# Attention with a routed feed-forward layer on one core: a sum of the first plan stands later on VectorE, and the plan's last steps and four scatters of the fifth batch stand at the end of pair 29

## The chip, the cores and the metric

The kernel runs on one core of a Trainium2 chip. The metric is the device time in microseconds (us) of one execution. Next to it stands a profile of one execution: which engine ran what, when, and what it waited for.

## What is computed

The reference, cut to what matters:

```python
def _attn_ref(q, k, v):                      # (8 batches, 8 heads, 576 tokens, 64), float32
    q_rot, k_rot = rotate(q), rotate(k)      # rotary embedding
    scores = np.matmul(q_rot, k_rot.transpose(0, 1, 3, 2)) / np.sqrt(D)
    attn = softmax(scores)
    return np.matmul(attn, v)

def _moe_ref(x, modality_id, w_gate, modality_bias, w1, w2):   # x: (4608, 512)
    logits = x @ w_gate + modality_bias[modality_id]           # 8 experts
    e_idx = np.argmax(logits, axis=1)                          # one expert for a token
    gate_w = softmax(logits)[np.arange(N), e_idx]
    for e in range(E):
        mask = e_idx == e
        h = np.maximum(x[mask] @ w1[e], 0.0)                   # w1[e]: 512 x 1024
        out[mask] = gate_w[mask, None] * (h @ w2[e])           # w2[e]: 1024 x 512
```

The attention's output, as 4608 rows of 512, is the input `x` of the second function.

## The kernel before

**Attention, 32 pairs.** Two heads are worked on together, so there are 32 pairs, and four pairs make a batch: pairs 16 to 19 are the fifth batch (number 4). For each pair the two rotated halves of q and k are loaded into one of two buffers `R` (`ST1` for even pairs, `ST2` for odd ones; the profile calls both ST), GpSimd multiplies them with cosine and sine and adds them (`rope_`, parts 0 to 2, lines 466 to 470), ScalarE rounds the sum to a high part (part 3, the HI step, a copy at L457) and GpSimd subtracts this to get the low part (part 4, the LO step, L474). Both stand in `HL`. Two copies for each of the two parts then write the other order of the two heads to `SW` (`swap`, L482): four DMAs for a pair, two that need HI and two that need LO. TensorE multiplies scores from `HL` and `SW` (L497), VectorE takes row minima and moves the scores out of PSUM (L506), ScalarE makes exponentials (L515), TensorE transposes them (L520), VectorE and ScalarE copy them out (L553 and L457), and TensorE multiplies them with V (L578). Even and odd pairs have a buffer each for `HL`, `SW`, `R` and V, so pair 31 takes the buffers that pair 29 had.

**Routing.** After the last pair of a batch, `route` finds each token's expert and its row in the expert's part of a DRAM table `XS`. The batch's output rows, in DRAM as `X`, are loaded back in five pieces (`back`, written BK0 to BK4, L761 and L763) into two buffers `XL`, used in turn, and each piece is scattered to `XS` by an indirect DMA that GpSimd issues (`scatter`, SC0 to SC4, L743). Since there are two buffers, the third load waits until the first scatter has read its buffer. For the first five batches the loads stand in SyncE's queue, for later ones in GpSimd's.

**The first plan.** When five batches are scattered, `plan0` decides which blocks of 512 rows are complete for an expert, and five blocks are worked off while the other batches are still being routed. The plan is a chain of small operations on one partition. Most are GpSimd's; its sums (`total`, L788) are VectorE's. `plan0` is a generator, cut by `yield` into steps.

**Experts.** The rows of a block are loaded (`m_ix`, `m_rows`), transposed and multiplied with the two weight matrices (`m_l1`, L1089; `m_plain`, `m_super`; L1207 and L1331). From there on TensorE works without a break to the end.

**What sets the order.** Each step is an entry of a list with a number; the list is sorted by it, and the engines' instructions are written in that order. The number of a step of pair n is 14.438 n plus an entry of the tables `KEYS` and `EDGE[n]`; that of a step of the expert part is 14.438 times 31 plus an entry of `MOE`. The numbers set the order alone; every engine runs its own row of instructions strictly in this order and waits where a buffer or a value is not there. SyncE issues nearly all loads, in the same order. So an instruction that waits holds up all that stands behind it on its engine.

Of the kernel before, what the change touches and what calls it, by code (L numbers as in the profile page):

```python
# [25 lines left out]
NSB = 4  # L26
NA = 1 + NSA
NB_MAX = 20
# [102 lines left out]
        "LD1": -42.214,  # L131
    },
    19: {
        "BK0": 71.4, "BK1": 71.5, "BK3": 95.0, "BK2": 116.0, "BK4": 131.0,
        "SC3": 113.825, "SC2": 128.215, "SC4": 152.075,
    },
# [73 lines left out]
    setdma=(-399.9101, -371.7589, -36.5660, -104.6596),  # L210
    consts=(-3.3332, 30.1765),
    plan=(-34.727, -25.884, -5.857, 16.183),
    ix=(-13.525, 11.679, 11.775, 17.3),
    w1=(-33.501, -27.735, 15.231, -22.655),
    w2=(-4.011, 1.762, 12.647, -8.483),
    hi=(-22.046, 1.027, 19.87, 16.903),
# [8 lines left out]
    l1d=(22.8091, 22.8691, 24.6621, 24.6471),  # L225
    w1n=(20.502, 24.643, 23.254, 22.825),
    place=(14.247, 18.005),
    rows=(-13.5, 11.7, 20.6, 31.756, 31.757),
    pl=(-114.356, -102.856, -99.906, -88.406, -85.506, -73.956, -51.417, -48.907, -45.303),
    end=24.98,  # L230
)
PIN = "PE,Activation,DVE,Pool"
# [3 lines left out]
def tile_attention_moe(ctx: ExitStack, tc: tile.TileContext, qk, v, mod, wg, mb, w1, w2, rope, cf, ci, out):  # L236
# [19 lines left out]
    PLA = cst.tile([1, 3, NA], I32, name="PLA")  # L256
    PLB = cst.tile([1, 3, NSB + NB_MAX + 1], I32, name="PLB")
# [6 lines left out]
    def cview(name):  # L264
        o, n = CF_OFF[name]
        return CF[:, o:o + n]
# [121 lines left out]
    def setup():  # L388
        g = nc.gpsimd
        v_ = nc.vector  # L390
        v_.memset(EPS, 1e-9)
        v_.memset(ZERO, 0.0)
        for t in PD:
            v_.memset(t, 0.0)
        v_.memset(P4, 0.0)
        for t in Vs:
            v_.memset(t[64:128, 0, 4, :], 0.0)
            v_.memset(t[0:64, 1, 4, :], 0.0)
        v_.memset(G, 0.0)
        for t in HL + SW:  # L400
            for c in (0, TW - 64):
                v_.memset(t[:, :, c:c + 64].bitcast(F32), 0.0)
        for h in range(4):
            for s in range(2):
                g.tensor_copy(RW[s * 64:s * 64 + 64, h, :].rearrange("p (o c) -> p o c", o=2)[:, :, 0:32],
                              idf[s * 64:s * 64 + 64, s * 64:s * 64 + 64].rearrange("p (o c) -> p o c", o=2))
        g.memset(MI, 0)
        nonlocal TI
        TI = XG[0].rearrange("p t g f -> p (t g f)")[:, 0:XU]
        g.memset(TI, 0.0)  # L410
        for x in XL:
            g.memset(x[:, XU:XW], 0.0)
        g.memset(TI[:, DM:DM + 1].bitcast(I32), EMPTY)
        g.memset(ON, 1.0)
        g.memset(OH, 0.0)
        g.dma_start(out=CF, in_=cf)
        g.dma_start(out=VAL, in_=ci)
# [363 lines left out]
    def plan0():  # L781
        G_ = nc.gpsimd

        def t1(name, sh):
            return sm.tile([1] + sh, F32, name=name, tag=name, bufs=1)

        def total(o, i):
            nc.vector.tensor_reduce(o, i, op=ALU.add, axis=AX.X)  # L788

        most = NPL * S // SUP  # L790
        AB = AB9[:, 0:E]
        sl = cview("SL")[0:1]
        EBv = cview("EB")[0:1]
        tri = cview("TRI")[0:1].rearrange("p (a b) -> p a b", b=E)
        nf, nb, cum, ge, tk, a2, rem, hc = (t1(x, [E]) for x in ("nf", "nb", "cum", "ge", "tk", "a2", "rem", "hc"))
        G_.tensor_tensor(nf, RUN[0:1, NPL, :], EBv, op=ALU.subtract)
        th = t1("th", [most])
        G_.tensor_scalar(th, sl[:, 0:most], float(SUP), float(SUP), op0=ALU.mult, op1=ALU.add)
        full = t1("full", [E, most])
        sh = [1, E, most]  # L800
        G_.tensor_tensor(full, nf.unsqueeze(2).to_broadcast(sh), th.unsqueeze(1).to_broadcast(sh), op=ALU.subtract)
        G_.tensor_scalar(full, full, 0.0, None, op0=ALU.is_ge)
        yield
        total(nb, full)
        yield
        t88 = t1("t88", [E, E])
        G_.tensor_tensor(t88, tri, nb.unsqueeze(1).to_broadcast([1, E, E]), op=ALU.mult)
        total(cum, t88)
        yield
        G_.tensor_tensor(tk, cum, nb, op=ALU.subtract)  # L810
        G_.tensor_scalar(tk, tk, float(NSA), None, op0=ALU.min)
        G_.tensor_scalar(a2, cum, float(NSA), None, op0=ALU.min)
        G_.tensor_tensor(a2, a2, tk, op=ALU.subtract)
        G_.tensor_scalar(hc, a2, float(SUP), None, op0=ALU.mult)
        G_.tensor_tensor(rem, nf, hc, op=ALU.subtract)
        G_.tensor_scalar(rem, rem, float(BLK), None, op0=ALU.is_ge)
        G_.tensor_tensor(t88, tri, rem.unsqueeze(1).to_broadcast([1, E, E]), op=ALU.mult)
        yield
        total(tk, t88)
        yield  # L820
        G_.tensor_scalar(tk, tk, 1.0, None, op0=ALU.is_equal)
        G_.tensor_tensor(rem, rem, tk, op=ALU.mult)
        G_.tensor_scalar(AB, a2, 2.0, None, op0=ALU.mult)
        G_.tensor_tensor(AB, AB, rem, op=ALU.add)
        sh = [1, NSA + 1, E]
        cmp = t1("cmp", [NSA + 1, E])
        cs = cmp[:, 1:NSA + 1, :]
        shs = [1, NSA, E]
        G_.tensor_tensor(cs, cum.unsqueeze(1).to_broadcast(shs), sl[:, 0:NSA].unsqueeze(2).to_broadcast(shs), op=ALU.subtract)
        G_.tensor_scalar(cs, cs, 0.0, None, op0=ALU.is_le)  # L830
        G_.tensor_tensor(cmp[:, 0, :], rem, cview("W8")[0:1], op=ALU.mult)
        yield
        es = t1("pes", [NB_MAX + 1])[:, 0:NA]
        total(es, cmp)
        yield
        G_.tensor_scalar(es[:, 0:1], es[:, 0:1], -1.0, float(E), op0=ALU.mult, op1=ALU.add)
        G_.tensor_scalar(es, es, float(E - 1), None, op0=ALU.min)
        G_.tensor_copy(PLA[:, 0, 0:NA], es)
        ch = t1("ch", [NB_MAX])[:, 0:NSA]
        G_.tensor_tensor(ch, es[:, 1:NA], es[:, 0:NSA], op=ALU.subtract)  # L840
        G_.tensor_scalar(ch, ch, 0.0, None, op0=ALU.is_equal)
        G_.tensor_scalar(PLA[:, 2, 1:NA], ch, -1.0, 1.0, op0=ALU.mult, op1=ALU.add)
        G_.memset(PLA[:, 2, 0:1], 1)
        G_.tensor_scalar(ge, nb, -float(SUP), float(RS), op0=ALU.mult, op1=ALU.add)
        G_.tensor_tensor(cs, cs, ge.unsqueeze(1).to_broadcast(shs), op=ALU.mult)
        G_.tensor_tensor(hc, hc, EBv, op=ALU.add)
        G_.tensor_scalar(hc, hc, float(-E * RS), None, op0=ALU.add)
        G_.tensor_tensor(cmp[:, 0, :], hc, rem, op=ALU.mult)
        yield
        rb = t1("rb", [NB_MAX])[:, 0:NA]  # L850
        total(rb, cmp)
        G_.tensor_scalar(rb[:, 0:1], rb[:, 0:1], float(E * RS), None, op0=ALU.add)
        r2 = t1("r2", [NB_MAX])[:, 0:NSA]
        G_.tensor_scalar(r2, sl[:, 0:NSA], float(SUP), None, op0=ALU.mult)
        G_.tensor_tensor(rb[:, 1:NA], rb[:, 1:NA], r2, op=ALU.add)
        G_.tensor_scalar(PLA[:, 1, 0:NA], rb, float(E * RS), None, op0=ALU.min)
        e2 = t1("e2", [NSB + 1])
        G_.tensor_scalar(e2[:, 0:1], es[:, NA - 1:NA], 1.0, None, op0=ALU.add)
        G_.memset(PLB[:, 2, NSB + NB_MAX:NSB + NB_MAX + 1], 1)
        G_.memset(CP9[:, 0:1], 0.0)  # L860
        G_.memset(AB9[:, E:E + 1], 0.0)
        G_.tensor_scalar(EB9, sl[:, 0:E + 1], float(RS), None, op0=ALU.mult)
        G_.tensor_scalar(EBN, EBv, float(-E * RS), None, op0=ALU.add)
        planned_[0] = e2
        yield
# [614 lines left out]

    K = KEYS
    setup()
    pinned = {getattr(mybir.EngineType, x) for x in PIN.split(",")}
    order = ExitStack()
# [62 lines left out]
    def Z(nm, i, f, *a):  # L1547
        J(MOE[nm][i], "moe", z, f, *a)
# [10 lines left out]
    for i in range(2):  # L1559
# [3 lines left out]
        Z("te", i, m_tre, 0, i, 0)  # L1563
        Z("ted", i, m_tre, 0, i, 1)
    g = plan0()
    for i in range(9):
        Z("pl", i, next, g, None)
    end = MOE["end"]
    for i, (s, j) in enumerate(((0, 0), (1, 0), (1, 1), (2, 0), (2, 1))):
# [186 lines left out]
```

## Time and profile before

| | |
|---|---|
| time, median of 3 runs | 871.61 us (868.73 to 873.98) |
| the profiled execution: its time, its span | 869.71 us, 867.9 us |
| TensorE busy (matmuls) | 833.6 us, 96% of the span |
| VectorE, ScalarE, GpSimd busy | 709.0, 611.8 and 460.3 us |
| granted TensorE clock, mean over the span | 0.996 |

The span runs from the first to the last instruction; the time is 1.8 us more. A busy share is an average over the whole span, which says little here: attention ends at about 460 us, the experts follow, and the change moves instructions between 360 and 440 us. There the rows of single waits have to be read.

### The profile page before, as it was taken

What the parts mean: (1) busy time and instruction counts of PE and PEld (TensorE: products, weight loads), DVE (VectorE), ACT (ScalarE), POOL (GpSimd) and SP (SyncE); (2) the same over time, 40 slices, a digit from 0 to 9 for tenths busy, and PEclk for the clock granted to TensorE, in tenths of its full rate; (3) what the DMA queues carried; (4) which work ended last, traced back from release to release, by engine and by line L of the source; (5) the groups of instructions that cost most, each with busy time, mean ns of one, the idle gap of its engine ahead of it and who ended that gap; (6) DMA issues with size and microseconds to landing.
All of it is one profiled execution on the core that took longest, in us unless ns stands there. A gap on an engine that the chain in (4) does not pass through costs nothing.

```text
span 867.9 us, 24887 instructions
## 1 busy us (share of the span) xinstructions
PE 833.6 (96%) x9528; PEld 689.5 (79%) x9528; DVE 709.0 (82%) x1595; ACT 611.8 (70%) x1311; POOL 460.3 (53%) x372
## 2 busy tenths in 40 slices
PE   2999999999999999899999999999999999999996
PEld 2777777777777777676778989898989898989895
DVE  7788898888888888797898677989898989897562
ACT  2898889898898988796985536565656575656453
POOL 3999979989999899899513123023302020202021
PEclk9999999999999999999999999999999999999999
DMA  8776858969789696875867983357964512531340
GB/s 289 211 242 180 272 158 261 265 203 266 217 257 272 201 276 192 259 223 173 233 197 195 332 227 107 61 179 227 298 173 153 139 50 49 172 97 49 121 142 22
DMA packets 115499, 165.81 MB, mean 191 GB/s; under 512 B 30636, under 2 KB 76350, under 8 KB 115372
## 3 DMA queue, kind: packets, MB, share of 16 engines
q1 hardware_dynamic: 106204, 137.99, 55.4%
q0 software_dynamic: 7824, 24.53, 8.2%
q8 instruction: 77, 1.26, 0.6%
q10 hardware_dynamic: 1344, 1.62, 0.6%
q14 instruction: 50, 0.41, 0.2%
HBM read 118.14 MB, written 34.70 MB: 176 GB/s over the span
## 4 chain that ended last, share of the span: by engine, by line
PE 46%; DVE 2%; POOL 1%; ACT 1%; issue 1%; SPq 1%; DMA 1%; POOLq 0%; ACTq 0%; DVEq 0%
PE psY L1331 20%; PE psH L1207 14%; PE ps L578 2%; PE psY L1207 2%; PE ps L520 1%; PE ps L497 1%; PE psH L1089 1%; PE psY L1108 1%; DMA ST<-in_moe_w_dram 1%; PE ps L1089 1%; PE psH L1403 1%; PE psY L1427 1%; DVE W2L L454 1%; SPq L1035 0%; PE ps L613 0%
## 5 line engine op out<-in xcount | busy, mean ns | idle before, releaser
L506 DVE CUSTOM_DVE_ANT_1 sc<-ps,ZERO 128x576 f32<-128x576 f32 x288 | 206.9, 749 | 23.5 <-PE ps L497 10.1
L515 ACT ACTIVATE P<-sc,mn 128x576 f32<-128x576 f32 x256 | 195.6, 768 | 5.6 <-DVE mn L506 5.0
L497 PE MATMUL ps<-HL 64*128 64x288 f32 x960 | 170.2, 312 | 12.5 <-ACT HL L457 11.3
L497 PE MATMUL ps<-SW 64*128 64x288 f32 x960 | 169.9, 312 | 4.2 <-DVE ST L468 3.6
L497 PEld LDWEIGHTS ps<-HL 64*128 64x128 f32 x960 | 136.3, 190 | 17.7 <-ACT HL L457 11.3
L1119 POOL DMA_INDIRECT out_dram<-sc,ix x36 | 43.8, 1218 | 200.2 <-ACT sc L1118 192.9
L497 PEld LDWEIGHTS ps<-SW 64*128 64x128 f32 x960 | 136.2, 190 | 8.8 <-DVE ST L468 3.9
L578 PE MATMUL ps<-PH,AT 128*64 128x320 f32 (+1 forms) x1024 | 138.2, 412 | 3.8 <-DVE PH L553 3.6
L1207 PE MATMUL psH<-HL,W1H 128*128 128x256 f32 x600 | 126.4, 279 | 0.2 <-ACT HL L457 0.2
L1207 PE MATMUL psH<-HL,W1L 128*128 128x256 f32 x400 | 111.6, 279 | 0.0
L578 PEld LDWEIGHTS ps<-PH,AT 128*64 128x64 f32 x1024 | 67.9, 136 | 52.0 <-DVE PH L553 7.0
L553 DVE COPY PH<-ps 128x512 f32<-128x512 f32 (+1 forms) x160 | 98.4, 631 | 10.0 <-PE ps L520 8.2
L457 ACT ACTIVATE PH<-ps 128x512 f32<-128x512 f32 (+1 forms) x160 | 85.1, 550 | 28.3 <-PE ps L520 23.2
L520 PEld LDWEIGHTS ps<-idf,P 64*128 64x128 f32 x2304 | 86.1, 138 | 21.9 <-ACT P L515 11.5
L1331 PE MATMUL psY<-W2L,SW 128*128 128x512 f32 x256 | 101.3, 396 | 0.0
L520 PE MATMUL ps<-idf,P 64*128 64x64 f32 x2304 | 97.6, 225 | 3.6 <-ACT AT L457 1.4
L1331 PE MATMUL psY<-W2H,SW 128*128 128x512 f32 x256 | 100.9, 394 | 0.0
L1207 PEld LDWEIGHTS psH<-HL,W1H 128*128 128x128 f32 x600 | 98.8, 188 | 1.0 <-ACT HL L457 0.4
L474 POOL TENSOR_TENSOR HL<-ST,HL 128x1152 fp32r<-128x1152 f32 x31 | 82.3, 2656 | 24.9 <-ACT HL L457 24.9
L743 POOL DMA_INDIRECT XS<-XL,oi x40 | 46.1, 1153 | 80.5 <-DMA XL<-X 60.6
L470 POOL TENSOR_TENSOR ST<-ST 128x1152 f32<-128x1152 f32 x30 | 79.7, 2656 | 1.2
L1207 PEld LDWEIGHTS psH<-HL,W1L 128*128 128x128 f32 x400 | 75.2, 188 | 0.0
(286 smaller groups left out, 1835.5 us busy)
## 6 DMA issues: line engine op xcount, KB each, us to landing
ST<-in_moe_w_dram SPq DMA_DIRECT2D x88, 512.0 KB
ST<-in_qk_dram SPq DMA_DIRECT2D x62, 576.0 KB
SW<-HL SPq DMA_DIRECT2D x124, 216.0 KB
AT<-in_v_dram SPq DMA_DIRECT2D x32, 256.0 KB
X<-X SPq DMA_DIRECT2D x8, 1024.0 KB
XL<-X SPq DMA_DIRECT2D x20, 257.0 KB
XG<-XS SPq DMA_DIRECT2D x40, 128.0 KB
XS<-ZR SPq DMA_DIRECT2D x8, 514.0 KB
```

The lines of the kernel that those rows point to most:

```text
L457: return nc.scalar.activation(o, i, AF.Copy, scale=scale)
L470: e.tensor_tensor(a, a, b, op=ALU.add)
L474: e.tensor_tensor(d["HL"][:, 1, o], a, d["HL"][:, 0, o].bitcast(F32), op=ALU.subtract)
L497: nc.tensor.matmul(ps[:, g, 0:288], t[:, wq, q0:q0 + P], t[:, wk, k0:k0 + 288], start=(m == 0), stop=(m == len(L) - 1))
L506: nc.vector.tensor_tensor_reduce(sc, d.pop(("S", u))[:, :, 0:288], ZERO.unsqueeze(2).to_broadcast([P, 2, 288]), 1.0, FMAX, ALU.add, ALU.mi ...
L515: nc.scalar.activation(p, sc.rearrange("p a b -> p (a b)"), AF.Exp, bias=mn, scale=-1.0, accum_out=d["sum"][:, u:u + 1])
L520: nc.tensor.transpose(ps[:, g, c:c + 64], src[r, k0:k0 + P], idf[r, r])
L553: alone(d["at", f], g, (nc.vector.tensor_copy if g else acopy)(o, i).ins, int(f[1] in "23B"))
L578: i = nc.tensor.matmul(pa[hh * 64:hh * 64 + 64, 0:c1 - c0], d["V"][:, hh, kt, :], r, start=(kt == 0), stop=(kt == 4))
L743: inst = nc.gpsimd.indirect_dma_start(out=XS, out_offset=bass.IndirectOffsetOnAxis(ap=oi[0:n, j:j + 1], axis=0), in_=xl[b, j][0:n], in_off ...
L1207: nc.tensor.matmul(ps[b][:, r * BLK:r * BLK + BLK], w[:, c, f0:f0 + P], x[:, c, :], start=(first and r == 0 and c == 0 and i == 0), stop=( ...
L1331: nc.tensor.matmul(po[t], hx[:, c, o:o + P], w[:, c, :], start=(k == 0 and c == 2 * q and i == 0), stop=(k == 3 and c == 2 * q + 1 and i = ...
```

## The change

The numbers of nine steps change, one step of the plan is cut in two, and two writes of a constant move. No operation is added or taken away, and no engine changes.

```diff
@@ EDGE[19], the fifth batch
-        "BK0": 71.4, "BK1": 71.5, "BK3": 95.0, "BK2": 116.0, "BK4": 131.0,
-        "SC3": 113.825, "SC2": 128.215, "SC4": 152.075,
+        "BK0": 71.4, "BK1": 71.5, "BK3": 95.0, "BK2": 156.0, "BK4": 156.1, "SC1": 151.5,
+        "SC3": 152.5, "SC2": 159.0, "SC4": 160.0,
@@ MOE
-    ix=(-13.525, 11.679, 11.775, 17.3),
+    ix=(-7.2, 11.679, 11.775, 17.3),
-    rows=(-13.5, 11.7, 20.6, 31.756, 31.757),
-    pl=(-114.356, -102.856, -99.906, -88.406, -85.506, -73.956, -51.417, -48.907, -45.303),
+    rows=(-7.0, 11.7, 20.6, 31.756, 31.757),
+    pl=(-114.356, -102.856, -99.906, -88.406, -82.0, -73.956, -51.417, -48.907, -45.303, -15.1),
@@ setup
         g.memset(ON, 1.0)
+        g.memset(PLA[:, 2, 0:1], 1)
@@ plan0
         G_.tensor_scalar(PLA[:, 2, 1:NA], ch, -1.0, 1.0, op0=ALU.mult, op1=ALU.add)
-        G_.memset(PLA[:, 2, 0:1], 1)
@@
         G_.tensor_scalar(PLA[:, 1, 0:NA], rb, float(E * RS), None, op0=ALU.min)
+        G_.memset(PLB[:, 2, NSB + NB_MAX:NSB + NB_MAX + 1], 1)
+        yield
         e2 = t1("e2", [NSB + 1])
         G_.tensor_scalar(e2[:, 0:1], es[:, NA - 1:NA], 1.0, None, op0=ALU.add)
-        G_.memset(PLB[:, 2, NSB + NB_MAX:NSB + NB_MAX + 1], 1)
@@
-    for i in range(9):
+    for i in range(10):
         Z("pl", i, next, g, None)
```

What this does to three engines' rows; TensorE's and ScalarE's are as they were. Lines of the changed kernel lie up to one further down, so its L475 is L474 of before, its L744 is L743, and its L483 is L482.

VectorE, in the work on pairs 25 and 26. `tk` is a sum of the plan over `t`, which GpSimd has to write; PH is a copy that TensorE's product with V needs, and the L506 rows are row minima of scores. Before:

```order
L506 ISA sc,mn<-ps_127,ZERO 128x576
L506 ISA mn 128x1
L788 TENSOR_REDUCE tk<-t_6810 1x8
L553 COPY PH_124<-ps_129 128x8x64
L506 ISA sc,mn<-ps_128,ZERO 128x576
```

And now:

```order
L554 COPY PH_124<-ps_129 128x8x64
L507 ISA sc,mn<-ps_128,ZERO 128x576
L507 ISA mn 128x1
L507 ISA sc,mn<-ps_127,ZERO 128x576
L507 ISA mn 128x1
L507 ISA sc,mn<-ps_126,ZERO 128x576
L507 ISA mn 128x1
L789 TENSOR_REDUCE tk<-t_6811 1x8
L675 TENSOR_REDUCE lg<-G 128x40
```

The copy and three minima now stand ahead of the sum.

GpSimd, from the plan's last steps to the LO step of pair 31, which writes HL_87. ST_74 is the rope of pair 30, ST_75 that of pair 31; the rows L858 to L863 are the plan's tail, and each DMA row is a scatter. Before:

```order
L856 TENSOR_SCALAR PLA<-rb 1x5
L858 TENSOR_SCALAR e_7850<-pes 1x1
L859 MEMSET PLB 1x1
L860 MEMSET CP_147 1x1
L861 MEMSET AB_145 1x1
L862 TENSOR_SCALAR EB_146<-CF 1x9
L863 TENSOR_SCALAR EBN<-CF 1x8
L466 TENSOR_TENSOR ST_74<-ST_74 128x1152
L743 DMA XS<-XL_83,oi 39424x528
L468 TENSOR_TENSOR ST_74<-ST_74,ST_75 128x1152
L470 TENSOR_TENSOR ST_74<-ST_74 128x1152
```

And now, further down in the same row of instructions:

```order
L471 TENSOR_TENSOR ST_75<-ST_75 128x1152
L744 DMA XS<-XL_83,oi 39424x528
L744 DMA XS<-XL_82,oi 39424x528
L668 COPY G<-XT 64x2x4x4
L860 TENSOR_SCALAR e_8509<-pes 1x1
L861 MEMSET CP_147 1x1
L862 MEMSET AB_145 1x1
L863 TENSOR_SCALAR EB_146<-CF 1x9
L864 TENSOR_SCALAR EBN<-CF 1x8
L744 DMA XS<-XL_83,oi 39424x528
L475 TENSOR_TENSOR HL_87<-ST_75,HL_87 128x1152
L744 DMA XS<-XL_82,oi 39424x528
```

The tail and the scatters SC1, SC3 and SC2 now stand between the last rope step of pair 31 (L471) and its LO step (L475), and SC4 behind that.

SyncE, from the load of V for pair 30 to that for pair 31. SW_89 is the swapped copy of pair 31, L1012 and L1035 are the index and row loads of the first block. Before:

```order
L358 DMA AT<-in_v_dram 128x2x256
L361 DMA AT<-in_v_dram 64x64 x2
L482 DMA SW_89<-HL_87 64x864 x4
L1012 ISA
L1012 DMA ix<-XS 128x2x2
```

And now:

```order
L358 DMA AT<-in_v_dram 128x2x256
L361 DMA AT<-in_v_dram 64x64 x2
L762 DMA XL_83<-X 128x514
L764 DMA XL_82<-X 64x514
L483 DMA SW_89<-HL_87 64x864 x4
L358 DMA AT<-in_v_dram 128x2x256
L361 DMA AT<-in_v_dram 64x64 x2
L1045 ISA
L1045 DMA ST_75<-in_moe_w_dram 128x2x512
L1013 ISA
L1013 DMA ix<-XS 128x2x2
```

The loads BK2 and BK4 now stand just ahead of the swaps of pair 31, and the first block's loads behind one load of V and one of weights.

## Rows read from the trace of the kernel before

**Rows 1.** Page: the engines' busy time, share of the span, instructions.

```profile
PE 833.6 (96%) x9528; PEld 689.5 (79%) x9528; DVE 709.0 (82%) x1595; ACT 611.8 (70%) x1311; POOL 460.3 (53%) x372
```

**Rows 2.** Busy time in stretches of 10 us; columns stand in the first line.

```profile
core 0: us, PE busy (x) PEld busy (x) DVE busy (x) ACT busy (x) POOL busy (x), PEclk, DMA share, GB/s
360.00:370.00 10.00, 7.22 (x118) 5.32 (x116) 6.65 (x19) 7.13 (x18) 9.22 (x14) 1.00 0.95 283
...
410.00:420.00 10.00, 8.61 (x174) 6.90 (x170) 7.74 (x24) 8.87 (x23) 9.92 (x5) 1.00 0.44 107
420.00:430.00 10.00, 10.00 (x152) 7.96 (x152) 8.31 (x22) 9.78 (x22) 5.26 (x4) 1.00 0.99 308
```

**Rows 3.** TensorE's waits between 300 and 560 us: total, times, longest.

```profile
PE ps L578 <- DVE PH L553: 2.8, 1, 2.8
PE ps L520 <- ACT AT L457: 1.4, 1, 1.4
```

**Rows 4.** VectorE in order of time, 356 to 372 us: start, duration, instruction, [idle before].

```profile
363.12 0.21 DVE L788 TENSOR_REDUCE tk<-t 1x8 f32<-1x64 f32 x1 [2.75 <-POOL t L817]
363.26 0.67 DVE L553 COPY PH<-ps 128x512 f32<-128x512 f32 x1
363.86 0.73 DVE L506 CUSTOM_DVE_ANT_1 sc<-ps,ZERO 128x576 f32<-128x576 f32 x1
...
371.21 0.14 DVE L685 TENSOR_REDUCE vm<-vv 128x5 f32<-128x40 f32 x1
```

**Rows 5.** GpSimd in order of time, 360 to 426 us.

```profile
362.78 0.31 POOL L817 TENSOR_TENSOR t<-CF,rem 1x64 f32<-1x64 f32 x1
...
366.01 1.06 POOL L743 DMA_INDIRECT XS<-XL,oi  x1 [0.17 <-issue]
...
370.50 0.28 POOL L682 TENSOR_TENSOR vv<-vv,CF 128x40 f32<-128x40 f32 x1
...
400.65 0.21 POOL L858 TENSOR_SCALAR e<-pes 1x1 f32<-1x1 f32 x1
...
401.56 2.64 POOL L466 TENSOR_TENSOR ST<-ST 128x1152 f32<-128x1152 f32 x1
...
418.80 2.64 POOL L470 TENSOR_TENSOR ST<-ST 128x1152 f32<-128x1152 f32 x1
...
425.70 2.67 POOL L474 TENSOR_TENSOR HL<-ST,HL 128x1152 fp32r<-128x1152 f32 x1 [2.95 <-ACT HL L457]
```

**Rows 6.** ScalarE in order of time: the HI step of pair 30.

```profile
410.93 1.16 ACT L457 ACTIVATE HL<-ST 128x1152 fp32r<-128x1152 f32 x1 [3.31 <-POOL ST L470]
```

**Rows 7.** SyncE's queue in time: XL's load; end of V for pair 30; swaps.

```profile
345.49 0.81 SPq L761 DMA_DIRECT2D XL<-X  x2
...
428.94 1.16 SPq L361 DMA_DIRECT2D AT<-in_v_dram  x2
430.19 2.47 SPq L482 DMA_DIRECT2D SW<-HL  x4
```

**Rows 8.** GpSimd in order of time: scatters that waited for a load, and one such load.

```profile
349.02 1.02 POOL L743 DMA_INDIRECT XS<-XL,oi  x1 [2.18 <-DMA XL<-X]
...
484.40 0.59 POOL L761 DMA_DIRECT2D XL<-X  x1
492.02 0.99 POOL L743 DMA_INDIRECT XS<-XL,oi  x1 [7.03 <-DMA XL<-X]
```

**Rows 9.** DMA traffic from 430 to 437 us, in 40 slices of 0.175 us.

```profile
GB/s 203 301 380 286 133 66 60 46 263 257 158 237 197 138 356 375 355 237 277 217 316 237 217 311 257 276 316 60 4 5 60 73 248 287 96 20 12 79 184 272
```

**Rows 10.** TensorE in order of time: pair 31's first scores.

```profile
437.26 0.38 PE L497 MATMUL ps<-SW 64*128 64x288 f32 x1
```

**Rows 11.** Stretches of 1 us early in the span; columns as in rows 2.

```profile
27.00:28.00 1.00, 0.38 (x4) 0.41 (x6) 1.00 (x2) 1.00 (x3) 0.92 (x2) 0.89 0.89 350
28.00:29.00 1.00, 1.00 (x12) 1.00 (x11) 0.35 (x3) 1.00 (x5) 1.00 (x1) 0.50 0.54 210
...
31.00:32.00 1.00, 1.00 (x23) 1.00 (x23) 0.36 (x3) 0.91 (x1) 0.02 (x1) 0.91 0.80 203
```

## The prediction

> **What bounds the kernel now.** I read the page first: TensorE is busy for 96% of the span, so the time is TensorE's work plus its few waits [rows 1]. Next come the stretches of 10 us around the places that the change touches. In most of them TensorE is busy all 10 us; in 360:370 and 410:420 it is not, while GpSimd is busy for 9.2 and 9.9 of the 10 us [rows 2]. The waits of TensorE name the two holes: 2.8 us for a copy of VectorE's and 1.4 us for one of ScalarE's [rows 3]. Everything the change can win in front lies in these two, and about as much can be lost, because a matmul delayed at 440 us delays the end by the same amount: behind 460 us TensorE works on with hardly a wait.
>
> **The first hole** starts on GpSimd. VectorE stood still for 2.75 us before the sum `tk`, until GpSimd had written `t`, and the copy that TensorE wanted stood behind it [rows 4, 5]. With the copy and three minima (0.6 and 3 x 0.68 us by the starts of the rows, together 2.6 us) ahead of the sum, they fill the wait: VectorE reaches `tk` at about 363.1, when `t` (362.78 + 0.31) is there. The scores of those minima were in PSUM already, since the minima ran back to back right behind the copy while TensorE was only starting on the product that the copy had released. This gives 2.75 us to VectorE and 2.8 to TensorE. What is late next is `vm`, a reduction over `vv` of GpSimd's. It ran at 371.21, 0.43 us after `vv` was written [rows 4, 5]. VectorE now comes to it at 368.5, while GpSimd, which loses one scatter (SC1, 1.06 + 0.17 us) ahead of `vv`, has it ready only at 369.55. So VectorE waits 1.1 us there and keeps 1.65. TensorE keeps between 1.65 and 2.8 us, as it has some scores in hand.
>
> **The second hole** is the HI step of pair 30. ScalarE stood still for 3.31 us, until GpSimd's rope of pair 30 was done [rows 6], and TensorE waited for a copy that stood behind it; its 1.4 us began some 1.9 us into ScalarE's wait. GpSimd comes there sooner by what leaves its row: SC1, SC3 and SC2 at 1.23 us each (1.06 + 0.17 at SC1), the memset of 0.1 us, and the plan's tail, 401.56 - 400.65 = 0.9 us [rows 5]: 4.7 us in all. ScalarE comes 1.65 to 2.8 us sooner, so of its 3.31 us at most 1.4 are left, and these are fewer than the 1.9 that TensorE had in hand. The hole closes: 1.4 us.
>
> In front that is 3.0 to 4.2 us; I take 3.5.
>
> **What is added, and where it stands.** The tail and the four scatters cost GpSimd the same as before, now between the rope of pair 31 and its LO step. That looks free: GpSimd had nothing to do from 422.7 to 425.7 but wait for ScalarE, and 420:430 has it busy for only 5.3 us [rows 2, 5]. The price is not the issue time but the wait of SC2. It sends the buffer that BK2 fills, and BK2 now stands in SyncE's queue behind the load of V for pair 30. Behind SC2 on GpSimd stands LO of pair 31; behind that, in SyncE's queue, the four swaps; and for these TensorE waits with the first scores of pair 31. Step by step:
>
> - Rope of pair 31 done: 418.80 + 2.64 - 4.7 = 416.7 [rows 5]. SC1 and SC3 follow to 419.2, a copy of 0.2 and the tail of 0.9 to 420.3. From there GpSimd waits for BK2.
> - BK2: before, SyncE was through with V for pair 30 at 428.94 + 1.16 = 430.1 [rows 7]. This load needs a buffer that TensorE frees, and the queue ahead of it needs GpSimd's LO of pair 30, so it comes sooner by 3.5 to 4.7 us; I take 4.1 and issue BK2 at 426.0. The buffer that it fills is free: SC1 was issued some nine us earlier.
> - Its landing is not shown at this place. The bounds: a load of the same size from the same queue let its scatter start 3.5 us after its issue began (345.49 to 349.02) [rows 7, 8]; one from GpSimd's queue took 7.6 us (484.40 to 492.02) [rows 8]. I take 4.5, nearer to the first because queue and size are the same, but more, because 420:430 has the DMA engines 0.99 busy [rows 2]. So SC2 starts at 430.5 and its issue ends at 431.6.
> - LO of pair 31: 2.67 us [rows 5], done at 434.3. Before it was done at 425.70 + 2.67 = 428.4, and SyncE came to the swaps only at 430.19 [rows 7].
> - Swaps: before, issued from 430.19 on; the traffic falls to 4 and 5 GB/s at 434.9 [rows 9], so they had landed 4.7 us after the first issue. Now: 439.0. The first scores need two of the four, so I let them start 0.6 us sooner, at 438.4.
> - TensorE before: product with V of pair 29, four transposes, first scores of pair 31 at 437.26 without a wait [rows 10]. Now it is ready at 437.26 - 3.5 = 433.8 and stands still for 4.6 us.
>
> The sum: -3.5 in front, +4.6 before pair 31, so **+1.1 us**. The gain is spent by the wait that takes its place. With the bounds of BK2's landing it is +0.1 (3.5 us) to +4.2 (7.6 us), and with those of its issue (425.4 or 426.6) 0.6 us less or more. The front's size hardly enters: what TensorE gains there it waits away.
>
> The Trainium skill gives a fixed part of about 2.0 us and 436 KB per us for a DMA on GpSimd's path (DMA: Bandwidth & Descriptors, "Anatomy of one DMA — SWDGE (gpsimd) path"). For BK2's 257 KB this makes an estimate of 2.6 us where the nearest row has 3.5, and with it the sum would be -0.8 us instead of +1.1.
>
> **What hides the rest.** The first block's index and row loads move from behind the swaps (430.19 + 2.47) to about 439.6, behind the swaps (434.3 + 2.5) and the loads of V and of weights (some 2.8 us, an estimate by the 1.16 us of two small loads of V [rows 7]), and need SC4, which follows LO at once. The transposes that use the rows stand in the expert part, past 450 us, so some 10 us cover them. The plan's tail is read by the second plan, past 540 us. BK2 and BK4 no longer hold SyncE near 381 and 391, where the swaps behind them waited anyway.
>
> **Rivals.**
>
> - *The gain survives* (chance 0.2). If BK2 is issued and lands sooner, LO ends sooner, and each us is one of TensorE's. To keep all of 3.5 us, LO would have to end by 429.7, so BK2 would have to land at 425.9, where I issue it. Half of it is possible: a landing of 2.5 us and an issue 0.6 sooner give -1.5. Center: 2 us faster, 869.6.
> - *The scatter's wait runs long* (0.13): slower. If BK2 lands as late as the slowest row, 7.6 us after its issue, TensorE stands still for 7.7 us and the sum is +4.2. A pause that long may also drop its clock: early in the span, with TensorE busy for 0.38 of the microsecond 27:28, the granted clock fell to 0.50 (1.2 of 2.4 GHz); the means 0.89 and 0.91 of the microseconds in which it fell and rose put that at 27.8 to 31.2 [rows 11], and 3.4 us at half speed lose 1.7 us. Together +5.9, 877.5. It decides from a landing of 6.1 us on, if the clock falls. The Trainium skill says that an idle TensorE is put back to 1.2 GHz and is let up to 2.4 GHz by activity (TensorE: Matmul & The Clock Gate, "Part 1: The HAM clock gate"); by that rule the fall comes. The trace agrees for the early stretch, but the 2.8 us pause at 361 us left the clock at 1.00 [rows 2, 3].
> - *The clock falls at the pause that I forecast* (0.12): +1.1 + 1.7 = +2.8, 874.4.
> - *The sum of the plan still stops VectorE*: if a bank for the three minima is not full, the wait stays in part. Then the front gives 1.4 us less or so, and the wait before pair 31 becomes shorter by the same: no other end. I give it no chance of its own.
>
> The forecast itself has 0.55.
>
> **The numbers.** The profiled execution took 869.71 us, and +1.1 makes 870.8; the median of the three runs is 1.9 us above it, so I predict 871.61 + 1.1 = 872.7. For the range: the first rival's center, less 1.6 us for the scatter of runs, makes 868.0; the third rival and the lower part of the second, with the same allowance, make 876.5. About 0.5%, or 4.4 us, is what a measurement of this kernel can tell from no change. Faster by more needs more than the whole front gain: 0.05. Slower by more needs the second rival: 0.12. The rest, 0.83, is within.
>
> **What the profile after would show.** Right: no wait of VectorE before `tk`, one of about 1 us before `vm`; none of TensorE for PH near 361 or for AT near 408; GpSimd waiting for the XL load before the third of the moved scatters, from about 420 to 430; a wait of TensorE of 3 to 6 us for SW, or for the LO step, before the first scores of pair 31, at about 434 to 438. Wrong: pair 31's scores starting near 434 without a wait (the first rival), or after 441 or at half clock (the second). It would also be wrong if VectorE's wait at `vm` grew until it cost TensorE the first hole again, or if the first block's rows came too late for their transposes.

## The result, and the profile after

| | before | after |
|---|---|---|
| time, median | 868.97 us (866.65 to 873.98, 19 runs) | 875.33 us (871.80 to 878.85, 19 runs) |
| ratio | | 1.0067, 95% interval 1.0052 to 1.0082 |
| the profiled execution: time, span, mean clock | 869.71, 867.9 us, 0.996 | 875.46, 873.7 us, 0.991 |

The changed kernel is slower, by 0.67% or 5.8 us by the ratio (the two medians lie 6.4 us apart). The time lies inside the predicted range (868.0 to 876.5), but beyond the 0.5% within which the prediction saw it with a chance of 0.83; slower by more had 0.12. That it lies inside the range is in part luck: the range was counted from 871.61 us, the median of three runs, and the median of 19 runs is 868.97. As ratios, the forecast is 1.0013 and the range ends at 1.0056; the measured 1.0067 is above it, though its interval reaches down to 1.0052.

TensorE's waits between 300 and 565 us, in the profile after (total, times, longest):

```profile
PE ps L498 <- DMA SW<-HL: 7.8, 2, 7.5
PE ps L579 <- DVE PH L554: 1.6, 1, 1.6
PE psH L1208 <- ACT HL L458: 1.3, 1, 1.3
```

The two waits of [rows 3] are gone (the 1.6 us for PH fall ahead of 355 us). In their place stands one of 7.5 us for the swapped copy SW. Stretches of 10 us show the same, and one thing more:

```profile
core 0: us, PE busy (x) PEld busy (x) DVE busy (x) ACT busy (x) POOL busy (x), PEclk, DMA share, GB/s
360.00:370.00 10.00, 9.91 (x156) 7.39 (x154) 9.28 (x28) 9.28 (x23) 9.25 (x16) 1.00 0.94 292
410.00:420.00 10.00, 10.00 (x176) 7.61 (x174) 9.69 (x28) 9.53 (x25) 9.23 (x11) 1.00 0.74 216
420.00:430.00 10.00, 10.00 (x150) 7.79 (x148) 7.43 (x23) 9.62 (x27) 0.14 (x1) 1.00 0.86 261
430.00:440.00 10.00, 2.47 (x22) 1.11 (x19) 2.35 (x7) 3.35 (x9) 5.82 (x8) 0.76 0.47 133
440.00:450.00 10.00, 9.99 (x148) 8.74 (x150) 6.62 (x20) 4.68 (x14) 0.75 (x3) 0.72 0.62 169
```

Against [rows 2], TensorE is busy for 9.91 instead of 7.22 us in 360:370 and for 10.00 instead of 8.61 in 410:420. Then GpSimd is busy for 0.14 us in 420:430, where it had 5.26, and TensorE for 2.47 us in 430:440. The granted clock is 0.76 and 0.72 in the last two stretches. At half clock (1.2 of 2.4 GHz, 0.50) that makes (0.24 + 0.28) x 10 / 0.5 = 10.4 us. The microseconds in which it fell and rose:

```profile
435.00:436.00 1.00, 0.00 (x0) 0.00 (x0) 0.00 (x0) 0.00 (x0) 0.90 (x3) 0.64 0.42 97
445.00:446.00 1.00, 1.00 (x34) 0.92 (x28) 0.97 (x5) 0.84 (x3) 0.47 (x2) 0.74 0.62 128
```

So it fell near 435.3, in the middle of the wait, and rose near 445.5. TensorE had work from 440.0 on: some 5.5 us of it ran at half speed, which loses about 2.8 us.

The first hole, on VectorE in order of time:

```profile
360.83 0.69 DVE L554 COPY PH<-ps 128x512 f32<-128x512 f32 x1
361.43 0.75 DVE L507 CUSTOM_DVE_ANT_1 sc<-ps,ZERO 128x576 f32<-128x576 f32 x1
...
363.46 0.20 DVE L789 TENSOR_REDUCE tk<-t 1x8 f32<-1x64 f32 x1
...
369.03 0.14 DVE L686 TENSOR_REDUCE vm<-vv 128x5 f32<-128x40 f32 x1
```

The copy runs at 360.83 instead of 363.26, and the sum `tk` at 363.46 with no wait [rows 4]. `vm`, which was forecast to wait some 1.1 us, has no wait either. The second hole, the HI step of pair 30 on ScalarE, has 1.46 us left of 3.31 [rows 6]:

```profile
405.81 1.17 ACT L458 ACTIVATE HL<-ST 128x1152 fp32r<-128x1152 f32 x1 [1.46 <-POOL ST L471]
```

What spends all of it is best seen in the chain of waits, in order of time from 425 to 450 us (start, duration, what; each piece is released by the one above it):

```profile
424.86 0.52 SPq L361
...
426.11 3.86 DMA XL<-X
...
430.74 1.04 POOL XS L744
...
431.81 2.62 POOL HL L475
...
434.45 0.50 SPq L483
...
435.68 4.19 DMA SW<-HL
...
440.01 2.65 PE ps L498 x15
```

It reads as a sentence: SyncE ends the load of V for pair 30 (L361), issues BK2 (`XL<-X`), which lands after 3.86 us; the scatter SC2 (L744) starts, then LO of pair 31 (L475), then the swaps (L483), whose landing lets TensorE begin pair 31's scores. On GpSimd and TensorE themselves (the last line is the experts' first matmul):

```profile
419.90 0.23 POOL L864 TENSOR_SCALAR EBN<-CF 1x8 f32<-1x8 f32 x1
430.74 1.04 POOL L744 DMA_INDIRECT XS<-XL,oi  x1 [10.60 <-DMA XL<-X]
431.81 2.62 POOL L475 TENSOR_TENSOR HL<-ST,HL 128x1152 fp32r<-128x1152 f32 x1
```

```profile
432.13 0.34 PE L521 MATMUL ps<-idf,P 64*128 64x64 f32 x4
440.01 0.58 PE L498 MATMUL ps<-SW 64*128 64x288 f32 x1 [7.54 <-DMA SW<-HL]
...
465.14 0.50 PE L1090 MATMUL ps<-HL,W1H 128*128 128x256 f32 x2
```

and in before, where the scores followed at 437.26 [rows 10]:

```profile
437.11 0.34 PE L520 MATMUL ps<-idf,P 64*128 64x64 f32 x4
...
459.82 0.50 PE L1089 MATMUL ps<-HL,W1H 128*128 128x256 f32 x2
```

So TensorE came to the transposes 4.98 us sooner and started the scores 2.75 us later.

**Where the time went, by one ruler.** The matmuls stand in the same order in all these kernels, so four of them mark three stretches: a product with V (319.75 us in before), the four transposes ahead of pair 31 (437.11), the first matmul of the experts (459.82), and one at the experts' steady part (572.69). The table has how much longer than in before each stretch was, in the one profiled execution of each kernel, beside the ratio of the timed runs. (After: 319.24, 432.13, 465.14, 578.58; so 112.89 - 117.36 = -4.5 in the first stretch, and so on.)

| kernel | front | pair 31 and the end of attention | start of the experts | ratio to before, 95% interval |
|---|---|---|---|---|
| after | -4.5 | +10.3 | +0.6 | 1.0067 (1.0052 to 1.0082) |
| SC2 behind LO | -5.6 | +3.4 | +1.4 | 0.9947 (0.9922 to 0.9972) |
| the same, once more | -3.3 | 0.0 | +2.9 | 0.9969 (0.9944 to 0.9995) |
| sum alone | +0.3 | 0.0 | +0.9 | 0.9989 (0.9963 to 1.0016) |
| after without the sum | -2.0 | +8.3 | +0.1 | 1.0096 (1.0066 to 1.0126) |
| filled wait | -4.2 | +8.6 | -1.6 | 1.0045 (1.0019 to 1.0070) |
| loads behind the swaps | -4.1 | +2.5 | +2.4 | 1.0006 (0.9983 to 1.0029) |
| BK2 early | -4.1 | +4.0 | +2.3 | 0.9997 (0.9973 to 1.0021) |
| SC2 behind LO, no sum | -4.1 | +3.6 | +2.6 | 1.0006 (0.9980 to 1.0032) |
| early loads, LO first | -3.9 | +5.3 | +1.3 | 1.0024 (0.9999 to 1.0048) |
| the same, no sum | -3.5 | +7.9 | +2.2 | 1.0037 (1.0008 to 1.0066) |

For after, 10.3 us in the second stretch are the wait of 7.54 and about 2.8 us lost by work at half clock. Executions of one kernel differ by some us among themselves (the first mark, ahead of everything that moves, lies between 319.1 and 324.3 us in these profiles), so a row of the table tells which stretch lost, and the ratio by how much the kernel is slower.

### The profile page after: what moved, and what is told of

Its sections match the earlier page's. It is cut to its first block, busy times and chain, and to the rows that moved or that the text cites. A ratio compares the mean times of both kernels' runs of the same rounds, so it can differ in the third digit from the quotient of the medians.

```text
span 873.7 us, 24883 instructions
## 1 busy us (share of the span) xinstructions
PE 834.1 (95%) x9528; PEld 690.4 (79%) x9528; DVE 708.4 (81%) x1595; ACT 611.7 (70%) x1311; POOL 460.1 (53%) x372
## 4 chain that ended last, share of the span: by engine, by line
PE 76%; DMA 6%; POOL 6%; issue 4%; ACT 3%; DVE 2%; SPq 1%; ACTq 0%; POOLq 0%; DVEq 0%
PE psY L1332 20%; PE psH L1208 14%; PE ps L579 13%; PE ps L498 13%; PE ps L521 8%; PE ps L614 2%; PE psY L1208 2%; DMA SW<-HL 2%; DMA XL<-X 2%; POOL HL L475 2%; PE psH L1090 1%; PE psY L1109 1%; ACT P L516 1%; POOL ST L469 1%; DMA ST<-in_rope_dram 1%
## 5 line engine op out<-in xcount | busy, mean ns | idle before, releaser
L475 POOL TENSOR_TENSOR HL<-ST,HL 128x1152 fp32r<-128x1152 f32 x31 | 82.4, 2659 | 21.1 <-ACT HL L458 21.0
L744 POOL DMA_INDIRECT XS<-XL,oi x40 | 46.2, 1155 | 89.4 <-DMA XL<-X 65.4
L471 POOL TENSOR_TENSOR ST<-ST 128x1152 f32<-128x1152 f32 x30 | 79.7, 2656 | 1.2
```

The source lines that it names most:

```text
L471: e.tensor_tensor(a, a, b, op=ALU.add)
L475: e.tensor_tensor(d["HL"][:, 1, o], a, d["HL"][:, 0, o].bitcast(F32), op=ALU.subtract)
L744: inst = nc.gpsimd.indirect_dma_start(out=XS, out_offset=bass.IndirectOffsetOnAxis(ap=oi[0:n, j:j + 1], axis=0), in_=xl[b, j][0:n], in_off ...
```

## The experiments

Three groups of kernels (1 to 4, 5 to 7, 8 to 10), each run on one chip beside the kernel before. Each edit is to the changed kernel unless it says otherwise.

**1. SC2 behind LO.** The chain is cut where it enters GpSimd: the scatter may wait, but LO and the swaps don't stand behind it.

```diff
-        "SC3": 152.5, "SC2": 159.0, "SC4": 160.0,
+        "SC3": 152.5, "SC2": 159.5, "SC4": 160.0,
```

> The changed kernel with one number changed: scatter SC2 stands behind the LO step of pair 31 on GpSimd instead of ahead of it. Theory A (the wait of SC2 for the load BK2 holds up LO, LO holds up the swaps, the swaps hold up TensorE): LO follows ScalarE's HI step and ends near 423.5 instead of 434.4, the swaps are issued from about 427 behind BK4, TensorE waits at most 1.5 us before pair 31's first scores, its clock stays up, and the time is 3 to 5 us under that of before (ratio 0.994 to 0.997). Rival B (the swaps are late because the loads BK2 and BK4 stand ahead of them in the same queue and share its traffic): the wait stays at 4 us or more and the time at or above before (1.000 to 1.005). Rival C (the loss lies in the expert part, in the first block's later index and row loads): no change against the changed kernel, 1.006.

Ratio 0.9947 (0.9922 to 0.9972): one number turned a kernel 0.67% slower into one 0.53% faster than before (0.31% in experiment 9). Theory A's ratio came, and those of the other two are excluded; its times were too early, for LO ended at 427.2 and not near 423.5. GpSimd in this kernel:

```profile
424.57 2.67 POOL L475 TENSOR_TENSOR HL<-ST,HL 128x1152 fp32r<-128x1152 f32 x1 [0.76 <-ACT HL L458]
434.88 1.06 POOL L744 DMA_INDIRECT XS<-XL,oi  x1 [7.64 <-DMA XL<-X]
```

SC2 still waits 7.6 us, but nothing that TensorE needs stands behind it. In this execution (the slowest of its twelve) the swaps left at 432.04, behind BK2 and BK4 in SyncE's queue, and TensorE waited for them twice, 1.3 and 1.5 us, where theory A had 1.5 at most.

**2. The sum alone.** The kernel before, with only the sum's number changed.

```diff
-    pl=(..., -88.406, -85.506, -73.956, ...),
+    pl=(..., -88.406, -82.0, -73.956, ...),
```

> The kernel before with only the sum tk moved behind the copy and three minima on VectorE. Theory A: the first hole of 2.8 us near 361 is gone and nothing is put in its place; the second hole near 411 grows by what TensorE and ScalarE come sooner to it, since GpSimd is not faster: between 0 and 2.8 us are left of the gain at the end (ratio 0.997 to 1.000), and the clock stays up. If GpSimd is what really sets the pace of this stretch, the second hole takes all of it back (wait of TensorE for AT near 411 of 4 us, ratio 1.000).

Ratio 0.9989 (0.9963 to 1.0016). The first hole is closed, 9.93 us busy in 360:370, but VectorE now waits for `vv`, and the second hole stays:

```profile
371.82 0.20 DVE L685 TENSOR_REDUCE vm<-vv 128x5 f32<-128x40 f32 x1 [1.33 <-POOL vv L682]
```

```profile
PE ps L520 <- ACT AT L457: 1.6, 1, 1.6
PE ps L520 <- DVE mn L506: 0.9, 1, 0.9
```

The wait at `vm`, which the prediction forecast for the whole change, comes here, where the scatters still stand in GpSimd's row ahead of the rope. By the table the front is 0.3 us longer than in before, so in this execution nothing of the gain is left. The timed runs cannot tell 0.9989 from 1.

**3. The change without the sum.** The rest of the change, with the sum back in its old place.

```diff
-    pl=(..., -88.406, -82.0, -73.956, ...),
+    pl=(..., -88.406, -85.506, -73.956, ...),
```

> The changed kernel with the sum tk back at its old place; all moves of scatters, loads and the plan's tail stay. Theory A (what TensorE gains in front it waits away before pair 31): the first hole is back at 2.8 us, the wait for the swaps is shorter by about as much (4 to 6 us instead of 7.5), pair 31's first scores start within 1 us of where they start in the changed kernel (near 440), and the time is that of the changed kernel within 2 us, less whatever a shorter pause saves of the clock (ratio to before 1.003 to 1.008). Rival: the moved sum itself costs the time; then this kernel is no slower than before (1.000 or under).

Ratio 1.0096 (1.0066 to 1.0126), above the expected 1.003 to 1.008. It is 0.0029 (2.5 us) above after, with intervals that overlap, so the expected difference of 2 us at most is not excluded either. The first hole is back with 2.2 us, and it was costlier than it looks:

```profile
360.00:370.00 10.00, 7.84 (x98) 4.96 (x98) 6.06 (x17) 6.11 (x16) 7.33 (x12) 0.83 0.90 290
...
436.00:446.00 10.00, 4.49 (x84) 4.39 (x84) 2.50 (x7) 1.09 (x5) 2.31 (x7) 0.66 0.78 205
```

The clock fell in the first hole too (0.83 is 3.4 us at half), and the chain before pair 31 ran with the same links: TensorE waited 6.7 us for SW there. It came to the transposes 2.4 us later than in after (434.49), and the wait, 0.9 us shorter, took back only that much of it: the swaps left at 435.98, 1.5 us later than in after, because GpSimd and SyncE also run later when the front does.

**4. The wait filled.** 96 matmuls on an old tile fill TensorE's wait, so that it does not stand still; they are extra work whose results are overwritten.

```diff
+        if n == NPAIR - 1 and u == 1:
+            for _ in range(48):
+                for g in range(2):
+                    t = HL[0][g * 64:g * 64 + 64]
+                    nc.tensor.matmul(ps[:, g, 0:288], t[:, 0, ...], t[:, 0, ...], start=True, stop=True)
```

> The changed kernel with 96 extra matmuls of pair 30's scores shape in front of pair 31's first scores, written to the bank that the first real matmul overwrites; they use data that is there and fit into the wait (48 steps of 0.13 us, 6.2 us). Theory A with the clock as a part of its own: the pause itself is as long, but TensorE is busy in it, the clock stays at 1.00, and the time falls by what the half clock cost, 2.5 to 3 us (half of the 5.5 us of work done at 0.50), to a ratio to before of 1.002 to 1.004. Rival (the clock's fall is not due to the pause, or costs nothing because other waits hide it): the time stays, 1.006 to 1.008.

Ratio 1.0045 (1.0019 to 1.0070). TensorE in order of time, and the stretches:

```profile
432.93 6.63 PE L497 MATMUL ps<-HL 64*128 64x288 f32 x96
441.06 0.40 PE L503 MATMUL ps<-SW 64*128 64x288 f32 x1 [1.50 <-DMA SW<-HL]
```

```profile
430.00:440.00 10.00, 9.56 (x121) 7.83 (x120) 2.99 (x9) 4.01 (x11) 5.87 (x8) 1.00 0.44 128
440.00:450.00 10.00, 8.86 (x164) 7.45 (x166) 7.65 (x23) 5.58 (x15) 0.75 (x3) 1.00 0.54 143
```

The clock stays at 1.00, and the scores still wait for SW until 441.06. The ratio lies between those of theory A and of the rival. It is lower than that of after by 0.0022, or 1.9 us; the two intervals overlap, so the runs alone do not settle the clock's share. The profiles put it at 2.1 to 2.8 us: from the first scores to the first matmul of the experts 22.56 us pass in before, 25.13 in after and 23.05 here, and 10.3 less 7.54 is 2.8. Either way the wait itself is the larger part.

**5. Both loads behind the swaps.**

```diff
-        ... "BK2": 156.0, "BK4": 156.1, ...
-        "SC3": 152.5, "SC2": 159.0, "SC4": 160.0,
+        ... "BK2": 159.7, "BK4": 159.75, ...
+        "SC3": 152.5, "SC2": 159.8, "SC4": 160.0,
```

> The changed kernel with BK2 and BK4 moved behind pair 31's swaps in SyncE's queue and SC2 behind LO of pair 31 on GpSimd, so that neither LO nor the swaps stand behind the load. Theory A (nothing but the chain BK2 - SC2 - LO - swaps spends the front's 5 us): GpSimd runs LO right behind the plan's tail or the copy of ScalarE's, the swaps leave some 4 us sooner than in the changed kernel and have landed when TensorE is through with the four transposes; TensorE does not wait before pair 31's first scores beyond 0.5 us, and the time is 5 to 7 us under before, ratio 0.992 to 0.995, at or below the version with SC2 alone moved (0.9947). Rival B (that version's remaining 2.8 us of waits have another cause, such as slow swaps): the two waits of 1.3 and 1.5 us stay and the ratio is 0.9945 to 0.996. Rival C (the scatters behind LO now hold the first block's index and row loads, and the expert part waits): a new wait past 440 us, ratio 0.997 or more.

Ratio 1.0006 (0.9983 to 1.0029): I expected the fastest version, and theory A is wrong here in its "nothing but". TensorE indeed does not wait for SW. But of the front's 4.1 us it loses 2.5 in pair 31, most of it in the routing's matmuls (L614), which stop twice for nothing that the profile shows. Another 2.4 us are lost behind 460 us, as theory C has it:

```profile
437.14 1.06 POOL L744 DMA_INDIRECT XS<-XL,oi  x1 [10.84 <-DMA XL<-X]
...
439.15 0.35 PE L614 MATMUL ps<-RW,AT 64*64 64x72 f32 x5 [0.36 <-issue]
...
443.56 0.71 SPq L1013 DMA_DIRECT2D ix<-XS  x1
...
468.09 1.22 DVE L455 TENSOR_TENSOR W1L<-ST,W1H 128x1024 fp32r<-128x1024 f32 x1 [4.86 <-ACT W1H L458]
...
474.03 0.85 PE L614 MATMUL ps<-RW,AT 64*64 64x72 f32 x36 [1.82 <-DVE XT L633]
```

(One row each, in this order, of GpSimd, TensorE, SyncE, VectorE and TensorE of this kernel.) BK2 was issued at 430.26 and let SC2 start only 6.9 us later; SC4 and the first block's index load follow. With that load at 443.56, weights that stand behind it in SyncE's queue come late, a split of weights on VectorE waits 4.9 us for them, and TensorE 1.8 us for a step behind that. That the index load's lateness is what starts it is read from the queue, not shown by a run of its own, and what stopped the routing's matmuls is open.

**6. BK2 early.** Ahead of the output loads and the load of V of pair 30; SC2 stays ahead of LO.

```diff
-        ... "BK2": 156.0, ...
+        ... "BK2": 151.6, ...
```

> The changed kernel with BK2 moved ahead of the output loads and the load of V of pair 30 in SyncE's queue, right behind the scatter that empties its buffer; SC2 stays ahead of LO. Theory A (each us by which BK2 lands sooner is one of TensorE's before pair 31): SyncE waits there for the scatter, BK2 lands at about 425 instead of 430.7, LO is done at about 429, the swaps land at about 434, TensorE stands still for 2 to 3 us instead of 7.5 and its clock does not fall; the load of V of pair 30 is late by at most 1 us. Ratio 0.996 to 1.000, between the version with SC2 behind LO and the kernel before. Rival B (SyncE's own standing costs as much: V of pair 30 or the swaps come late because the queue waits for the scatter): TensorE waits for V ahead of the product of pair 29 or 30, ratio 1.003 to 1.007.

Ratio 0.9997 (0.9973 to 1.0021), as theory A expected. SyncE stood for the scatter until 421.13, SC2 started at 424.56, the swaps at 428.60, and TensorE waited 1.8 us instead of 7.5. But the clock, which theory A kept up, fell after so short a wait as well (0.83 in 430:440), and pair 31 still cost 4.0 us. The stretch:

```profile
430.00:440.00 10.00, 8.09 (x122) 6.21 (x118) 6.48 (x19) 5.54 (x17) 2.94 (x9) 0.83 0.77 208
```

**7. SC2 behind LO, without the sum.** Experiment 1 with the sum back in its old place (the edit of experiment 3).

> The version with SC2 behind LO of pair 31, with the sum of the plan put back to its old place ahead of the three minima on VectorE. It leaves no long wait before pair 31 that could swallow the sum's gain, so the two versions differ by what the sum is worth. Theory A (the sum's move gives TensorE the first hole, some 2 to 2.8 us, and nothing behind takes it back): 2 to 3 us slower than the version with the sum moved, ratio 0.997 to 0.999, and TensorE waits some 2 us for a copy of VectorE's near 360 us again. Rival B (TensorE's first hole is given back anyway, by waits for the swaps or elsewhere): within 1 us of the version with the sum moved, ratio 0.994 to 0.996. Rival C (the pause at 360 us also drops the clock, as it did in the profile of the changed kernel without the sum's move): 4 to 5 us slower, ratio 0.999 to 1.001.

Ratio 1.0006 (0.9980 to 1.0032), above the 0.9947 and 0.9969 of its partner, which ran on other chips. TensorE waited 1.6 us for PH in the first hole, not 2.8:

```profile
363.56 0.21 DVE L789 TENSOR_REDUCE tk<-t 1x8 f32<-1x64 f32 x1 [1.54 <-POOL t L818]
```

The sum waits 1.5 us here where it waited 2.75 in before [rows 4]. No step has left GpSimd's row ahead of `t`, so the change does not explain the shorter wait. TensorE came to the hole 1.7 us later than in before, as late as it was at the table's first mark (321.51), while `t` came only 0.4 us later: the engines stand a little differently to each other in each execution. The ratio is that of rival C, but not for its cause: the clock was 1.00 in 360:370 and fell behind the wait of 1.4 us before pair 31 (0.92 and 0.91 in 430:440 and 440:450).

**8. Early loads and LO first.** Both cures at once: the loads right behind the scatters that empty their buffers, and the scatters that send them behind LO.

```diff
-        ... "BK2": 156.0, "BK4": 156.1, ...
-        "SC3": 152.5, "SC2": 159.0, "SC4": 160.0,
+        ... "BK2": 151.6, "BK4": 151.65, ...
+        "SC3": 151.55, "SC2": 159.5, "SC4": 160.0,
```

> The changed kernel with BK2 and BK4 right behind the scatters that empty their buffers (ahead of the output loads and of the load of V of pair 30 on SyncE), SC3 right behind SC1, and SC2 and SC4 behind LO of pair 31. Theory A (the chain of BK2, SC2, LO and the swaps is all that spends the front's gain): SyncE stands still for some 4 us for a scatter, but LO runs at about 422 to 425, the swaps follow the load of V at about 427 to 428 and have landed when TensorE needs them or up to 1 us later; SC2 and SC4 find their loads landed, the first block's indices come earlier than in the version with both loads behind the swaps, and TensorE does not wait for XT near 470. From before pair 31 to the expert part TensorE keeps 3 to 5 us of the front's gain; ratio 0.992 to 0.996, the fastest of these versions. Rival C (the gain is given back in the expert part, whatever stands before pair 31): TensorE keeps its lead up to 460 us and loses it again by 550 us in new waits for weights or XT; ratio 0.998 to 1.001.

Ratio 1.0024 (0.9999 to 1.0048): both theories missed. GpSimd had LO done at 426.4, yet TensorE waited 3.6 us for SW. SyncE's queue shows why:

```profile
422.30 0.34 SPq L762 DMA_DIRECT2D XL<-X  x1
425.25 0.47 SPq L764 DMA_DIRECT2D XL<-X  x1
...
428.65 1.64 SPq L358 DMA_DIRECT2D AT<-in_v_dram  x1
430.39 1.58 SPq L361 DMA_DIRECT2D AT<-in_v_dram  x2
432.06 3.10 SPq L483 DMA_DIRECT2D SW<-HL  x4
```

The scatters were issued at 417.93 and 419.33, and the loads into their buffers had to wait for each to end: 422.30 and 425.25. All that stands behind them in the queue came later, the swaps at 432.06. The wait was moved from GpSimd to SyncE, and the swaps stand behind it again. They were slow as well: the scores started 6.9 us after the first of them was issued, 5.56 in after.

**9. Experiment 1 once more,** on the chip of 8 and 10.

> The version with SC2 alone moved behind LO of pair 31, once more, beside the others on one chip. Theory A: as before, ratio 0.992 to 0.997. Rival (its first measurement was of a chip or an hour that suited it, and it stands with the versions that were measured beside each other later): 0.998 to 1.002.

Ratio 0.9969 (0.9944 to 0.9995): faster again. In this profile pair 31 takes nothing back. SyncE:

```profile
427.84 0.54 SPq L762 DMA_DIRECT2D XL<-X  x1
428.46 0.45 SPq L764 DMA_DIRECT2D XL<-X  x1
429.50 2.42 SPq L483 DMA_DIRECT2D SW<-HL  x4
```

and TensorE:

```profile
436.46 0.34 PE L521 MATMUL ps<-idf,P 64*128 64x64 f32 x4
436.61 0.38 PE L498 MATMUL ps<-SW 64*128 64x288 f32 x1
```

The scores follow the transposes at once, the clock stays at 1.00, and all 3.3 us of the front reach the experts. There 2.9 are lost: TensorE waits 2.0 us for OH, and the clock is 0.94 and 0.77 in 540:546 and 546:552, where before had 1.1 us and 1.00. So this execution, 871.10 us, is no faster than the profiled one of before, and the gain is told by the timed runs alone.

**10. Experiment 8 without the sum** (the edit of experiment 3).

> The version with early loads and LO first, with the sum of the plan put back to its old place on VectorE. Theory A (the sum's move is worth the first hole of TensorE, some 2 us, wherever no wait behind it swallows that): 1.5 to 3 us slower than the version with the sum moved, a difference of 0.002 to 0.0035 in the ratio. Rival B (the sum's move is worth nothing to the end): within 0.001 of it. Rival C (its pause near 360 us also drops the clock): 0.004 to 0.006 slower.

Ratio 1.0037 (1.0008 to 1.0066), 0.0013 above its partner: between theories A and B, and within the uncertainty. In four pairs (2 and before; 3 and after; 7 and 1 or 9; 10 and 8) the kernel with the sum moved is the faster one, by 0.0011, 0.0029, 0.0037 to 0.0059, and 0.0013. All four point the same way, but the intervals overlap in all but experiment 7 against 1, and those two were measured on different chips. So the sum seems to be worth 1 to 5 us; how much stays open.

## Why the prediction came out as it did

**Right: the mechanism and its place.** Both holes close, and a wait for the swaps before pair 31 takes their place through BK2, SC2, LO and the swaps. The times along this chain, forecast and measured: BK2 issued 426.0 and 426.11; SC2's start 430.5 and 430.74; LO done 434.3 and 434.43; swaps issued 434.3 and 434.45. BK2's landing was costed at 4.5 us between 3.5 and 7.6; it took 4.6 from issue to scatter (3.86 to the landing, in the chain above). That this hits so well is in part luck: the same load took 3.4 us in experiment 6 and 6.9 in experiment 5. The estimate of 2.6 us by the Trainium skill (DMA: Bandwidth & Descriptors, "Anatomy of one DMA — SWDGE (gpsimd) path"), a figure for GpSimd's path, was too short for this load of SyncE's in a stretch where the DMA engines were 0.86 busy. Experiments 1 and 9 show that SC2's place in this chain is what makes the change slower: with SC2 behind LO the rest of it is a gain.

**Mis-sized: the front's gain.** "In front that is 3.0 to 4.2 us; I take 3.5" measured 4.98 at the transposes (4.5 by the ruler). The 1.1 us at `vm` were subtracted in vain: GpSimd had written `vv` at 368.81, not at 369.55, and `vm` found it there at 369.03. Two shorter waits of TensorE in before, 0.28 us near 388 and 0.47 near 398, are gone too. One reading behind the second hole was wrong, without effect: TensorE's 1.4 us began at 411.08, 3.5 us into ScalarE's wait and not 1.9. In the sum the extra 1.5 us hardly enter, since they make the wait longer by the same amount; but that the front's size never matters is too strong, as in experiment 3 the chain moved along with it in part.

**Mis-sized: the swaps' landing.** "The first scores need two of the four, so I let them start 0.6 us sooner, at 438.4" failed. In the chain the third issue of the swaps (435.64) has a DMA of 4.19 us behind it, and the scores start 5.56 us after the first issue, not 4.1. In all eight kernels whose scores waited for the swaps, they started 5.5 to 6.9 us after the first issue, so 4.1 was too short everywhere: the fall of the traffic in before [rows 9] probably did not show the landing that TensorE waits for. In before the four were issued within 2.47 us [rows 7], here within 3.12; what else slowed them is open. The two terms make 4.6 + 1.5 + 1.5 = 7.6 of the wait, measured 7.54.

**Wrong: the likeliest case had full clock.** The sum let TensorE stand 4.6 us and go on at full speed, and left the clock to two rivals, together 0.25, at 1.7 us taken from a stretch of 3.4 us at half speed [rows 11]. It fell, for 10.4 us, and cost some 2.8 us by the profile of after (2.1 beside experiment 4). The Trainium skill's rule that an idle TensorE is put back to 1.2 GHz (TensorE: Matmul & The Clock Gate, "Part 1: The HAM clock gate") was cited for just that, and here the trace agrees: 0.50 from the middle of a wait of 7.54 us. With the wait at 7.54 and the clock's 2.8 against 4.5 to 5.0 in front, the sum is +5.3 to +5.8 instead of +1.1, and the two profiled executions lie 5.75 us apart. It is the price of the rival "the scatter's wait runs long" (+5.9), though not by its cause: the load's landing was nearly as forecast. The cause is that of the third rival, the clock's fall at the pause that was forecast (0.12), whose +2.8 had the swaps 1.5 us and the clock 1.1 us too cheap.

**Right: what was said to be hidden.** No wait of TensorE for the first block's rows is seen; its index load came at 440.63 (forecast 439.6). Only a wait of 1.3 us for a copy of ScalarE's at the experts' start is longer than in before, and the third stretch as a whole costs 0.6 us. In experiment 5 the same load came 2.9 us later and the experts waited, in experiment 3 it came 1.5 us later and they did not; whether the load is the cause in experiment 5 is not shown.

## What to carry to other kernels

A step that waits for a transfer is priced by what stands behind it on its queue, not by its own cost: here a scatter whose issue takes 1 us waited 10.6 us for its load and held LO, the swaps and, for 7.5 us, TensorE, and setting it one place further down gave 0.3 to 0.5% over the kernel before. Moving the wait to another queue (SyncE, experiments 6 and 8) made TensorE's wait shorter, 1.8 and 3.6 us, but gave no kernel faster than before, since the same swaps stand behind it there. A forecast pause of TensorE should be priced with the clock's fall as a case of its own, with the work behind it counted at half speed.

## What the runs showed of the hardware that was not expected

- A stretch at half clock was not always 3.4 us, as early in the span [rows 11]: after the pause of 7.54 us it made up 10.4 us, in experiment 3 6.8 us (0.66 in 436:446).
- The length of a pause alone did not tell whether the clock falls: 2.8 us at 361 us in before left it at 1.00 [rows 2, 3], and so did the two waits of 1.3 and 1.5 us in experiment 1, while 2.2 us at the same place in experiment 3 and 1.8 us in experiment 6 were followed by 0.83 in the stretch of 10 us.
- The same kind of load, BK2 from SyncE's queue, took 3.4 us to its scatter in experiment 6, 4.6 in after and 6.9 in experiment 5, where the swaps had been issued just ahead of it.
